# Attention's other TensorE work at fixed places, and each group's output projection in the group behind it

## The chip, the cores and the metric

The kernel runs on one NeuronCore of a Trainium2 chip. A core has five engines, each with its own queue of instructions in program order: PE (matrix multiply, with its weight loads shown apart as PEld), DVE (vector work), ACT (exp, gelu and copies), POOL (a second vector engine that cannot read PSUM), and SP, which here only issues DMA. Matmuls write PSUM, eight banks of 128 x 512 float32 numbers. The metric is the device time of one execution in microseconds; the time of a kernel is the median of its runs.

## The reference

One layer of 2048 tokens with 448 features. A gate per token mixes attention (16 heads of 28, one shared key and value head) with a shifted MLP block:

```python
def _A_ref(x, wq, wk, wv, wo):
    q = (x @ wq).reshape(B, S, H, Dh).transpose(0, 2, 1, 3)
    k = x @ wk
    v = x @ wv
    scores = jnp.einsum("bhqd,bkd->bhqk", q, k) * (Dh ** -0.5)
    p = _softmax(scores, axis=-1)
    o = jnp.einsum("bhqk,bkd->bhqd", p, v)
    return o.transpose(0, 2, 1, 3).reshape(B, S, H * Dh) @ wo

g = _sigmoid((x * gate_w).sum(-1, keepdims=True))
return g * _A_ref(x, wq, wk, wv, wo) + (1 - g) * _B_ref(x, w1, w2, w3, w4)
```

`_B_ref` is a layernorm, a product with w1, gelu, shifts of the tokens by one and two, a product with w2 and a sum with x, then a second layernorm and an MLP with w3 and w4.

## The kernel before, in words

The MLP block comes first and leaves its result in `x1`, already multiplied by 1 - g. The attention behind it is what the change touches.

Numbers that need full precision are split in a high and a low part of a rounded type (names ending in h and l); a product is then three matmuls. A **group** u is one of 16 pairs of a query block b (512 tokens) and a set g of four heads, u = 4b + g. For each group there are:

- **q**: `q_job` makes the queries of a group with 11 matmuls of 512 columns into one PSUM tile. `q_evac` then splits the tile (ACT copies `qh`, DVE subtracts to `ql`) and three DMAs on SP write them to `q_of[u]`.
- **m**: `max_part` makes scores of 128 keys only, four matmuls of 128 columns for one token tile t, and DVE takes their largest (L167). After four such sets `max_end` makes `mc` on DVE, and `max_rows` turns it with one matmul (`mt`), ACT copies it to `mrow`, and two small DMAs write it as further rows of `q_of[u]`, so that the score matmul subtracts it.
- **s and p**: for each of the 16 key tiles kt and each of the four heads j one matmul gives scores `s` (128 keys x 512 queries), and ACT takes exp of them to `p`.
- **pv**: `pv_group` adds the product of p with the values (and a column of ones) to one PSUM tile for the whole group. It is written for two key tiles at a time, behind the second of a pair, and with the p of the pair before (`LAG`, `PVB`). A float32 matmul shows as two records, so a pair has 16 of them.
- **norm**: when a group's pv is complete, `recip_begin` copies the tile to `o` (ACT), moves the row sums by DMA (`rt`), takes reciprocals on DVE and moves them back by two DMAs (`rb`). `norm_job` spreads them over the rows with one matmul (`rbc`), DVE multiplies, and POOL splits the product in `onh` and `onl`.
- **wo**: the output projection of a query block takes, for each token tile t and each of four groups g, three matmuls of 448 columns.

PE's order in attention is the order in which the program is written (the schedule of PE is manual); the other engines keep each its own queue, ordered by the framework. The loop over k runs through all key tiles of all groups, k = 16u + kt. Work that is not s, p or pv is a generator in the list `jobs`, and each call of `pump` writes one of its matmuls:

```python
if j % 2 == 1 or u == NU - 1:
    pump()
```

So `pump` (L600) is called twice in each key tile, in the last group four times. A q job is put ahead of the list at kt = 2 of each group (7 in the first); a norm job joins it six key tiles after its pv, and a block's four wo jobs (`wo_job`, L566) eight after the pv of its fourth group. A job's end takes a call of `pump` of its own. The m sets stand behind key tiles 6 to 9, `max_rows` behind 11 (L668 to L674).

`wo_job` adds all four groups of a block in one PSUM tile, 12 matmuls, and `gate_out` (L561) multiplies by the gate, adds `x1` and issues the output's DMA. For the last block this is done otherwise: `wo_last_job` (L638) keeps four PSUM tiles for its four token tiles over the whole last group, taken from the banks of `m_tile` and `s_more`, and adds groups 0 to 2 of the block into them during that group; the tail behind the loop adds the fourth.

PSUM in attention: two banks each for `mm_tile` and `s_more` and one for `s_spare` hold s in turn (in the last group only the first and the last of these, three banks: `s_tile`, L477), one bank holds pv, and two banks of `m_tile` serve q, m, mt, rbc and wo.

Of the kernel before, what the change touches and what calls it, by code (L numbers as in the profile page):

```python
# [8 lines left out]
F32 = mybir.dt.float32  # L9
F32R = mybir.dt.float32r  # L10
AF = mybir.ActivationFunctionType
ALU = mybir.AluOpType
# [3 lines left out]
P = 128  # L16
S = 2048
D = 448
# [4 lines left out]
NB = S // 512  # L23
NT = S // P
NF = F // P
NG = H // 4
# [14 lines left out]
def gated_mix_kernel(  # L41
# [13 lines left out]
    nc = tc.nc  # L55
# [11 lines left out]
    x1 = keep.tile([P, NT, D], F32, name="x1")  # L67
# [3 lines left out]
    gg = keep.tile([P, NT], F32, name="gg")  # L71
# [20 lines left out]
    def misc_tile(name):  # L92
        return psA.tile([P, 512], F32, tag="misc", bufs=1, name=name)
# [59 lines left out]
    NU = NB * NG  # L153
# [299 lines left out]
    with tc.tile_pool(name="s3", bufs=1, reuse_waits="tile") as s3, \  # L453
# [8 lines left out]
        woh = s3.tile([P, 4, D], F32R, name="woh")  # L462
# [11 lines left out]
        def s_spare(name):  # L474
            return psA.tile([P, 512], F32, tag="misc", bufs=1, name=name)

        def s_tile(n, last=False):  # L477
            return (mm_tile, mm_tile, s_spare, s_more, s_more)[n % (3 if last else 5)](f"s_{n}")

        xact = {}  # L480

# [10 lines left out]
        def q_job(u):  # L492
            b, g = divmod(u, NG)
            ah, al = xact[b]
            cols = slice(g * P, (g + 1) * P)
            ps = misc_tile(f"q_{u}")
            ops = []
            for c in range(3):
                ops += [(wqh[:, c, cols], ah[:, c, :]), (wqh[:, c, cols], al[:, c, :]), (wql[:, c, cols], ah[:, c, :])]
            ops += [(wqh[:, 3, cols], ah[:, 3, :]), (wql[:, 3, cols], ah[:, 3, :])]  # L500
            for n, (w, a) in enumerate(ops):
                nc.tensor.matmul(ps, w, a, start=(n == 0), stop=(n == 10))  # L502
# [10 lines left out]
        on_of = {}  # L513
# [23 lines left out]
            nc.sync.dma_start(f32(rb)[4:8, :].rearrange("j (a b) -> j a b", b=16), f32(rl))  # L537
            return o, rb

        def norm_job(u, o, rb):  # L540
            ps = (mm_tile if u == NU - 2 else misc_tile)(f"rbc_{u}")
            nc.tensor.matmul(ps, sel8, rb, start=True, stop=True)
            on = s3.tile([P, 512], F32, tag="onf", bufs=2, name=f"on_{u}")
            nc.vector.tensor_mul(on, o, ps)  # L544
            onh = s3.tile([P, 512], F32R, tag="onh", bufs=5, name=f"onh_{u}")
            onl = s3.tile([P, 512], F32R, tag="onl", bufs=5, name=f"onl_{u}")
# [5 lines left out]
        def wo_group(ps, b, t, g, first, last):  # L552
            tok = slice(t * P, (t + 1) * P)
            onh, onl = on_of[b * NG + g]
            nc.tensor.matmul(ps, onh[:, tok], woh[:, g, :], start=first, stop=False)  # L555
# [3 lines left out]
            nc.tensor.matmul(ps, onl[:, tok], woh[:, g, :], start=False, stop=last)  # L559

        def gate_out(n, ps):  # L561
            ot = s3.tile([P, D], F32, tag="ot", bufs=3, name=f"ot_{n}")
            nc.vector.scalar_tensor_tensor(ot, ps, gg[:, n:n + 1], x1[:, n, :], op0=ALU.mult, op1=ALU.add)  # L563
            nc.sync.dma_start(out[0, n * P:(n + 1) * P, :], ot)

        def wo_job(b, t):  # L566
            ps = misc_tile(f"wo_{b}_{t}")[:, 0:D]
            for g in range(NG):
                yield from wo_group(ps, b, t, g, g == 0, g == NG - 1)
                if g < NG - 1:  # L570
                    yield
            gate_out(4 * b + t, ps)
            yield

        wqraw = s3.tile([P, 4, 512], F32, tag="raw", bufs=2, name="wqraw")
        nc.sync.dma_start(wqraw, wq)
# [20 lines left out]
        jobs = []  # L597
        current = [None]

        def pump():  # L600
            if current[0] is None:
                if jobs:
                    current[0] = jobs.pop(0)()
                    next(current[0])
            else:
                try:
                    next(current[0])
                except StopIteration:
                    current[0] = None

        def drain():
            while current[0] is not None or jobs:
                pump()

        p_of, pv_of = {}, {}

        def pv_group(k):
            u, kt = divmod(k, NT)
            if kt == 0:
                pv_of[u] = max_tile(f"pv_{u}")  # L620
            pv = pv_of[u]
            ps = p_of.pop(k)
            for j in range(4):
                nc.tensor.matmul(pv[32 * j:32 * j + 32, :], vext[:, kt, :], ps[j],  # L624
                                 start=(kt == 0), stop=(kt == NT - 1), tile_position=(0, 32 * j))
            if kt == NT - 1 and u < NU - 1:
                o, rb = recip_begin(u, pv_of.pop(u))
                delayed.append((k + 6, lambda: norm_job(u, o, rb)))
                if u == NU - 2:
                    for t in range(4):  # L630
                        delayed.append((k + 10, lambda t=t: wo_last_job(t, NG - 2)))
                elif u % NG == NG - 1:
                    for t in range(4):
                        delayed.append((k + 8, lambda t=t: wo_job(u // NG, t)))

        wo_last = []

        def wo_last_job(t, g):  # L638
            if g == 0:
                wo_last.append((m_tile if t < 2 else s_more)(f"wo_{NB - 1}_{t}")[:, 0:D])  # L640
            yield from wo_group(wo_last[t], NB - 1, t, g, g == 0, False)
            yield

        delayed = []
        for k in range(NU * NT + LAG):
            u, kt = divmod(k, NT)
            while delayed and delayed[0][0] <= k:
                jobs.append(delayed.pop(0)[1])
            if k == (NU - 1) * NT:
                for g in range(NG - 2):  # L650
                    for t in range(4):
                        jobs.append(lambda t=t, g=g: wo_last_job(t, g))
            if k < NU * NT:
                if kt == (7 if u == 0 else 2) and u + 2 < NU:
                    jobs.insert(0, lambda u=u: q_job(u + 2))
                if kt == 8 and (u + 3) % NG == 0 and u + 3 < NU:
                    load_x((u + 3) // NG)
                p_of[k] = []
                for j in range(4):
                    n = 4 * k + j  # L660
                    ps = s_tile(n, u == NU - 1)
                    nc.tensor.matmul(ps, kS[0:98, kt * P:(kt + 1) * P], q_of[u][0:98, j, :], start=True, stop=True)  # L662
                    p = s3.tile([P, 512], F32, tag="p", bufs=4 * (LAG + PVB) + 2, name=f"p_{n}")
                    nc.scalar.activation(p, ps, AF.Exp, scale=SCALE)  # L664
                    p_of[k].append(p)
                    if j % 2 == 1 or u == NU - 1:
                        pump()
                if u + 1 < NU:  # L668
                    if 6 <= kt < 10:
                        max_part(u + 1, kt - 6, m_tile)  # L670
                    elif kt == 10:
                        max_end(u + 1)
                    elif kt == 11:
                        max_rows(u + 1, m_tile)  # L674
            if k >= LAG and k % PVB == PVB - 1:
                for kk in range(k - LAG - PVB + 1, k - LAG + 1):
                    if kk >= 0:
                        pv_group(kk)
        assert not delayed
        drain()  # L680

        u = NU - 1
        pv = pv_of.pop(u)
        o = s3.tile([P, 512], F32, tag="o", bufs=2, name=f"o_{u}")
        onh = s3.tile([P, 512], F32R, tag="onh", bufs=5, name=f"onh_{u}")
        onl = s3.tile([P, 512], F32R, tag="onl", bufs=5, name=f"onl_{u}")
        on_of[u] = (onh, onl)
        toks = [slice(t * P, (t + 1) * P) for t in range(4)]
        on4 = {}
# [15 lines left out]
            nc.vector.tensor_sub(onl[:, toks[t]], tq, f32(onh)[:, toks[t]])  # L705

        def tail_c(t):
            for _ in wo_group(wo_last[t], NB - 1, t, NG - 1, False, True):
                pass
            gate_out(4 * (NB - 1) + t, wo_last[t])  # L710

        for t in range(4):
            nc.scalar.copy(o[:, toks[t]], pv[:, toks[t]])
# [19 lines left out]
        with tc.If(again > 0):  # L733
            for b in range(NB):
                load_x(b)
                for g in range(NG):
# [7 lines left out]
                    for kt in range(NT):  # L744
                        for j in range(4):
# [7 lines left out]
                    for _ in norm_job(u, *recip_begin(u, pv, False)):  # L753
                        pass
                for t in range(4):
                    for _ in wo_job(b, t):
                        pass


_OUTS = [((1, S, D), "float32")]  # L760
# [48 lines left out]
```

## Time and profile before

| what | us |
|---|---|
| median of three runs | 1069.96 (1068.99 to 1070.19) |
| the profiled execution, its own time | 1067.96 |
| its span, first to last instruction | 1066.2 |
| PE busy in the span | 1040.3 |
| ACT busy in the span | 673.5 |
| attention, from the first s matmul to the end of the last pv | 420.57 to 1051.67 |

A line of a timeline has the start from the span's begin, the duration, engine, source line, operation, the tiles written and read, shapes, and the number of instructions that were merged; in brackets stands how long the engine was idle before it and what released it. A row of stretches has its limits and length, then for each of PE, PEld, DVE, ACT and POOL the busy time and (x) the number of instructions, then the clock that PE was granted, and the share and rate of DMA. A row of groups has busy time, mean duration in ns of one instruction, and the idle time before them with what ended it. Durations of matmuls overlap, so the time that a matmul takes of PE is read from start to start.

### The profile page before, as it was taken

The page shows a single profiled execution, that of the slowest core. Times are in us where ns is not written, and L with a number is a line of the kernel's source. Part 1 is how long each engine was busy: PE and PEld are TensorE (multiplying, and loading weights), DVE is VectorE, ACT ScalarE, POOL GpSimd, SP SyncE. Part 2 cuts the span into 40 slices and gives each one's busy share as a digit, 9 for nine tenths or more (in the row PEclk, how much of TensorE's full clock was granted, in tenths as well). Part 3 has the DMA queues.
Part 4 walks back from the last instruction along what each step waited for, and adds up shares of the span by engine and source line. Part 5 has one row for each costly group of instructions (what it writes and reads, how often), then busy time and mean ns, then how long its engine had stood idle before and what let it go on. Part 6 is the DMA issues. An engine that isn't in the chain of part 4 may idle for free.

```text
span 1066.2 us, 13945 instructions
## 1 busy us (share of the span) xinstructions
PE 1040.3 (98%) x5610; PEld 679.5 (64%) x5610; DVE 258.6 (24%) x528; ACT 673.5 (63%) x1318; POOL 146.1 (14%) x175
## 2 busy tenths in 40 slices
PE   7999989999999999999999999999999999999996
PEld 4787878888888887454554555554655555555442
DVE  6734862411412212301110110120110210111102
ACT  5444462222222223798888888889888888888873
POOL 5622200200200202602000002020002010000100
PEclk8899999999999999999999999999999999999998
DMA  9501330000000001323211202220202220202001
GB/s 312 133 1 37 112 111 1 1 1 1 1 1 1 1 1 61 132 32 70 32 18 15 31 19 41 39 31 3 39 10 41 39 31 2 40 21 30 10 2 38
DMA packets 30541, 41.15 MB, mean 39 GB/s; under 512 B 8004, under 2 KB 20100, under 8 KB 30340
## 3 DMA queue, kind: packets, MB, share of 16 engines
q1 hardware_dynamic: 30324, 40.04, 16.2%
q8 instruction: 46, 0.75, 0.3%
q14 instruction: 27, 0.22, 0.1%
q10 hardware_dynamic: 144, 0.13, 0.0%
HBM read 23.28 MB, written 3.67 MB: 25 GB/s over the span
## 4 chain that ended last, share of the span: by engine, by line
PE 92%; DVE 2%; DMA 2%; ACT 1%; POOL 1%; issue 1%; SPq 0%; POOLq 0%; DVEq 0%; ACTq 0%
PE s L662 27%; PE pv L624 22%; PE acc L418 4%; PE acc L419 4%; PE acc L420 4%; PE g L115 4%; PE g L116 4%; PE g L117 4%; PE q L502 3%; PE m L166 2%; PE wo L559 1%; PE wo L557 1%; PE g L119 1%; PE wo L555 1%; PE g L118 1%; PE h L116 1%
## 5 line engine op out<-in xcount | busy, mean ns | idle before, releaser
L664 ACT ACTIVATE p<-s 128x512 f32<-128x512 f32 x1024 | 517.6, 630 | 99.7 <-PE s L662 99.4
L662 PE MATMUL s<-qs,kS 98*128 98x512 f32 x1024 | 343.5, 420 | 1.4 <-ACT p L664 0.7
L662 PEld LDWEIGHTS s<-qs,kS 98*128 98x128 f32 x1024 | 181.7, 189 | 168.3 <-ACT p L664 126.2
L624 PE MATMUL pv<-p,vext 128*32 128x512 f32 x2048 | 247.5, 601 | 0.0
L408 ACT ACTIVATE gh<-g 128x512 fp32r<-128x512 f32 x56 | 33.6, 599 | 175.0 <-PE g L119 174.9
L624 PEld LDWEIGHTS pv<-p,vext 128*32 128x32 f32 x2048 | 53.7, 109 | 107.5 <-issue 100.1
L410 DVE TENSOR_TENSOR gl<-gf,gh 128x512 fp32r<-128x512 f32 x56 | 38.7, 692 | 183.8 <-ACT gf L409 183.8
L418 PE MATMUL acc<-w4h,gh 128*128 128x448 f32 x224 | 82.8, 370 | 0.0
L419 PE MATMUL acc<-w4l,gh 128*128 128x448 f32 x224 | 82.0, 366 | 0.0
L420 PE MATMUL acc<-w4h,gl 128*128 128x448 f32 x224 | 81.7, 365 | 0.0
L167 DVE TENSOR_REDUCE mr<-m 128x4 f32<-128x512 f32 x64 | 44.2, 691 | 146.8 <-PE m L166 146.1
L115 PE MATMUL g<-ah,w3h 128*128 128x512 f32 x168 | 66.6, 396 | 3.7 <-ACT gf L409 3.7
L116 PE MATMUL g<-al,w3h 128*128 128x512 f32 x168 | 66.3, 395 | 0.0
L117 PE MATMUL g<-ah,w3l 128*128 128x512 f32 x168 | 66.3, 394 | 0.0
L547 POOL CAST onh<-on 128x512 fp32r<-128x512 f32 x15 | 9.2, 614 | 415.0 <-DVE on L544 228.9
L520 DVE SCALAR_TENSOR_TENSOR good<-rt,good 128x16 f32<-128x16 f32 x15 | 2.6, 175 | 190.9 <-DMA rt<-o 190.9
L418 PEld LDWEIGHTS acc<-w4h,gh 128*128 128x128 f32 x224 | 42.2, 188 | 4.9
L419 PEld LDWEIGHTS acc<-w4l,gh 128*128 128x128 f32 x224 | 42.2, 188 | 4.9
L420 PEld LDWEIGHTS acc<-w4h,gl 128*128 128x128 f32 x224 | 42.0, 188 | 3.6
L166 PEld LDWEIGHTS m<-kS,qs 96*128 96x128 f32 x256 | 38.4, 191 | 6.3 <-DVE mr L167 1.2
L115 PEld LDWEIGHTS g<-ah,w3h 128*128 128x128 f32 x168 | 31.7, 188 | 9.9 <-ACT gf L409 4.1
L563 DVE SCALAR_TENSOR_TENSOR ot<-wo,gg,x 128x448 f32<-128x448 f32 x16 | 10.9, 681 | 108.0 <-PE wo L559 107.9
(204 smaller groups left out, 1134.9 us busy)
## 6 DMA issues: line engine op xcount, KB each, us to landing
qs<-qh SPq DMA_DIRECT2D x32, 256.0 KB
qs<-ql SPq DMA_DIRECT2D x16, 256.0 KB
xq<-in_xT_dram SPq DMA_DIRECT2D x4, 1024.0 KB
x<-in_x_dram SPq DMA_DIRECT2D x4, 896.0 KB
w3raw<-in_w_dram SPq DMA_DIRECT2D x7, 512.0 KB
out_dram<-ot SPq DMA_DIRECT2D x16, 224.0 KB
w4raw<-in_w_dram SPq DMA_DIRECT2D x7, 448.0 KB
xkv<-in_xT_dram SPq DMA_DIRECT2D x3, 1024.0 KB
```

Of the source, the lines that this page charges most:

```text
L115: nc.tensor.matmul(ps, wh[:, c, :], ah[:, c, :], start=(c == 0), stop=False)
L116: nc.tensor.matmul(ps, wh[:, c, :], al[:, c, :], start=False, stop=False)
L117: nc.tensor.matmul(ps, wl[:, c, :], ah[:, c, :], start=False, stop=False)
L166: nc.tensor.matmul(ps[:, j, :], q_of[u][0:96, j, t * P:(t + 1) * P], kS[0:96, 0:MK], start=True, stop=True)
L167: nc.vector.reduce_max(mx_of[u][:, :, t], ps, axis=AX.X)
L410: nc.vector.tensor_sub(gl, gf, f32(gh))
L418: nc.tensor.matmul(ps, gh[:, tok], w4h[i][:, k, :], start=(f == 0), stop=False)
L419: nc.tensor.matmul(ps, gh[:, tok], w4l[i][:, k, :], start=False, stop=False)
L420: nc.tensor.matmul(ps, gl[:, tok], w4h[i][:, k, :], start=False, stop=(f == NF - 1))
L624: nc.tensor.matmul(pv[32 * j:32 * j + 32, :], vext[:, kt, :], ps[j], start=(kt == 0), stop=(kt == NT - 1), tile_position=(0, 32 * j))
L662: nc.tensor.matmul(ps, kS[0:98, kt * P:(kt + 1) * P], q_of[u][0:98, j, :], start=True, stop=True)
L664: nc.scalar.activation(p, ps, AF.Exp, scale=SCALE)
```

## The change

`wo_job` now makes the projection of one group and one token tile, three matmuls in a PSUM tile of its own, and DVE adds the gated result to `ot` (the first group of a block adds to `x1`); the DMA of the output follows the fourth group. `wo_group`, `gate_out`, `wo_last_job` and the special case of the last block are gone, and s keeps its five banks to the end. Norm is no job any more but stands at key tile 6 of the next group, behind the second s. A job's last matmul no longer takes a further call of `pump`. `pump` is called at the places that `slots` names: behind the fourth s of every key tile and behind the second s of seven of them, 23 calls in a group, the number of 11 q and 12 wo matmuls. A group's q job starts at its key tile 0 (9 in the first group) and the wo jobs of the group before it at key tile 8. The m sets stand behind key tiles 3, 5, 7 and 9 and `max_rows` behind 11; in the first group behind 0, 1, 2, 3 and 6. PE's number of instructions is the same, DVE has 48 more for the adds in the part that runs. `onh` and `onl` have two buffers instead of five, `ot` five instead of three.

```diff
-        def s_tile(n, last=False):
-            return (mm_tile, mm_tile, s_spare, s_more, s_more)[n % (3 if last else 5)](f"s_{n}")
+        def s_tile(n):
+            return (mm_tile, mm_tile, s_spare, s_more, s_more)[n % 5](f"s_{n}")
...
-        def norm_job(u, o, rb):
-            ps = (mm_tile if u == NU - 2 else misc_tile)(f"rbc_{u}")
+        def norm(u, o, rb):
+            ps = misc_tile(f"rbc_{u}")
             nc.tensor.matmul(ps, sel8, rb, start=True, stop=True)
...
-        def wo_job(b, t):
-            ps = misc_tile(f"wo_{b}_{t}")[:, 0:D]
-            for g in range(NG):
-                yield from wo_group(ps, b, t, g, g == 0, g == NG - 1)
-                if g < NG - 1:
-                    yield
-            gate_out(4 * b + t, ps)
-            yield
+        def wo_job(u, t, tile_of=misc_tile):
+            b, g = divmod(u, NG)
+            n = 4 * b + t
+            tok = slice(t * P, (t + 1) * P)
+            onh, onl = on_of[u]
+            ps = tile_of(f"wo_{u}_{t}")[:, 0:D]
+            nc.tensor.matmul(ps, onh[:, tok], woh[:, g, :], start=True, stop=False)
             yield
             nc.tensor.matmul(ps, onh[:, tok], wol[:, g, :], start=False, stop=False)
             yield
+            nc.tensor.matmul(ps, onl[:, tok], woh[:, g, :], start=False, stop=True)
+            before = x1[:, n, :] if g == 0 else ot_of[n]
+            if g == 0:
+                ot_of[n] = s3.tile([P, D], F32, tag="ot", bufs=5, name=f"ot_{n}")
+            nc.vector.scalar_tensor_tensor(ot_of[n], ps, gg[:, n:n + 1], before, op0=ALU.mult, op1=ALU.add)
+            if g == NG - 1:
+                nc.sync.dma_start(out[0, n * P:(n + 1) * P, :], ot_of[n])
...
         def pump():
-            if current[0] is None:
-                if jobs:
-                    current[0] = jobs.pop(0)()
-                    next(current[0])
-            else:
-                try:
-                    next(current[0])
-                except StopIteration:
+            if jobs or current[0]:
+                current[0] = current[0] or jobs.pop(0)
+                if next(current[0], "done") == "done":
                     current[0] = None
...
+        def slots(u, kt):
+            if u == 0:
+                two = kt in (9, 11, 13, 15)
+                return () if kt < 9 else ((1, 3) if two else (3,))
+            return (1, 3) if kt in (0, 3, 7, 9, 11, 13, 15) else (3,)
+
+        def m_places(u):
+            return (0, 1, 2, 3, 6) if u == 0 else (3, 5, 7, 9, 11)
+
         for k in range(NU * NT + LAG):
             u, kt = divmod(k, NT)
...
+            if k < NU * NT:
+                if kt == (9 if u == 0 else 0) and u + 2 < NU:
+                    jobs.append(q_job(u + 2))
+                if kt == 8 and u > 0:
+                    for t in range(4):
+                        jobs.append(wo_job(u - 1, t))
...
-                    if j % 2 == 1 or u == NU - 1:
+                    if j in slots(u, kt):
                         pump()
-                if u + 1 < NU:
-                    if 6 <= kt < 10:
-                        max_part(u + 1, kt - 6, m_tile)
-                    elif kt == 10:
+                    if kt == 6 and j == 1 and norms:
+                        norm(*norms.pop())
+                if u + 1 < NU and kt in m_places(u):
+                    t = m_places(u).index(kt)
+                    if t < 4:
+                        max_part(u + 1, t, m_tile)
+                    else:
+                        max_rows(u + 1, m_tile)
+                    if t == 3:
                         max_end(u + 1)
-                    elif kt == 11:
-                        max_rows(u + 1, m_tile)
```

More of the change, by code (lines that the diff above doesn't have):

```diff
@@ L544, in norm_job @@
             nc.vector.tensor_mul(on, o, ps)
-            onh = s3.tile([P, 512], F32R, tag="onh", bufs=5, name=f"onh_{u}")
-            onl = s3.tile([P, 512], F32R, tag="onl", bufs=5, name=f"onl_{u}")
+            onh = s3.tile([P, 512], F32R, tag="onh", bufs=2, name=f"onh_{u}")
+            onl = s3.tile([P, 512], F32R, tag="onl", bufs=2, name=f"onl_{u}")
             nc.gpsimd.tensor_copy(onh, on)
@@ L549, in norm_job @@
             on_of[u] = (onh, onl)
-            yield
-        def wo_group(ps, b, t, g, first, last):
+        ot_of = {}
+        def wo_job(u, t, tile_of=misc_tile):
+            b, g = divmod(u, NG)
+            n = 4 * b + t
             tok = slice(t * P, (t + 1) * P)
-            onh, onl = on_of[b * NG + g]
-            nc.tensor.matmul(ps, onh[:, tok], woh[:, g, :], start=first, stop=False)
+            onh, onl = on_of[u]
+            ps = tile_of(f"wo_{u}_{t}")[:, 0:D]
+            nc.tensor.matmul(ps, onh[:, tok], woh[:, g, :], start=True, stop=False)
             yield
@@ L600, in pump @@
         def pump():
-            if current[0] is None:
-                if jobs:
-                    current[0] = jobs.pop(0)()
-                    next(current[0])
-            else:
-                try:
-                    next(current[0])
-                except StopIteration:
+            if jobs or current[0]:
+                current[0] = current[0] or jobs.pop(0)
+                if next(current[0], "done") == "done":
                     current[0] = None
[L611 to L615, printed above, removed]
+        p_of, pv_of, norms = {}, {}, []
         def pv_group(k):
@@ L626, in pv_group @@
             if kt == NT - 1 and u < NU - 1:
[L627 to L644, printed above, removed]
+                norms.append((u, *recip_begin(u, pv_of.pop(u))))
+        def slots(u, kt):
[5 more added lines that the diff above has]
+            return (0, 1, 2, 3, 6) if u == 0 else (3, 5, 7, 9, 11)
         for k in range(NU * NT + LAG):
             u, kt = divmod(k, NT)
[L647 to L650, printed above, removed]
+            if k < NU * NT:
+                if kt == (9 if u == 0 else 0) and u + 2 < NU:
+                    jobs.append(q_job(u + 2))
+                if kt == 8 and u > 0:
                     for t in range(4):
[L652 to L655, printed above, removed]
+                        jobs.append(wo_job(u - 1, t))
                 if kt == 8 and (u + 3) % NG == 0 and u + 3 < NU:
@@ L660, in gated_mix_kernel @@
                     n = 4 * k + j
-                    ps = s_tile(n, u == NU - 1)
+                    ps = s_tile(n)
                     nc.tensor.matmul(ps, kS[0:98, kt * P:(kt + 1) * P], q_of[u][0:98, j, :], start=True, stop=True)
@@ L678, in gated_mix_kernel @@
                         pv_group(kk)
-        assert not delayed
-        drain()
+        while current[0] or jobs:
+            pump()
+        assert not norms
         u = NU - 1
@@ L684, in gated_mix_kernel @@
         o = s3.tile([P, 512], F32, tag="o", bufs=2, name=f"o_{u}")
-        onh = s3.tile([P, 512], F32R, tag="onh", bufs=5, name=f"onh_{u}")
-        onl = s3.tile([P, 512], F32R, tag="onl", bufs=5, name=f"onl_{u}")
+        onh = s3.tile([P, 512], F32R, tag="onh", bufs=2, name=f"onh_{u}")
+        onl = s3.tile([P, 512], F32R, tag="onl", bufs=2, name=f"onl_{u}")
         on_of[u] = (onh, onl)
@@ L707, in tail_c @@
         def tail_c(t):
-            for _ in wo_group(wo_last[t], NB - 1, t, NG - 1, False, True):
+            for _ in wo_job(u, t, m_tile if t < 2 else s_more):
                 pass
-            gate_out(4 * (NB - 1) + t, wo_last[t])
         for t in range(4):
@@ L752, in gated_mix_kernel @@
                                              start=(kt == 0), stop=(kt == NT - 1), tile_position=(0, 32 * j))
[L753 to L757, printed above, removed]
+                    norm(u, *recip_begin(u, pv, False))
+                    for t in range(4):
+                        for _ in wo_job(u, t):
+                            pass
 _OUTS = [((1, S, D), "float32")]
```

7 lines of the change are left out of this document (removed).

## The prediction

> **What bounds the kernel now.** I read the page first, then busy time by stretch, then PE's timeline pair by pair.
>
> ```profile
> span 1066.2 us, 13945 instructions
> PE 1040.3 (98%) x5610; PEld 679.5 (64%) x5610; DVE 258.6 (24%) x528; ACT 673.5 (63%) x1318; POOL 146.1 (14%) x175
> ```
>
> PE looks full. The stretches below are group 0, groups 1 to 13 together, group 14 and group 15 up to its last pv matmul (a group is one u: 512 queries of four heads).
>
> ```profile
> 420.57:461.81 41.24, 39.36 (x206) 18.90 (x204) 12.59 (x16) 32.54 (x66) 21.76 (x16) 0.96 0.50 144
> 461.81:967.29 505.48, 505.48 (x3004) 274.19 (x3000) 72.89 (x165) 432.31 (x872) 42.75 (x33) 1.00 0.18 29
> 967.29:1005.69 38.40, 38.40 (x231) 20.30 (x227) 7.61 (x14) 32.64 (x66) 3.78 (x4) 1.00 0.04 14
> 1005.69:1051.67 45.98, 45.06 (x249) 20.96 (x245) 1.38 (x5) 32.92 (x66) 1.89 (x2) 1.00 0.01 1
> ```
>
> Attention is 631 of the 1066 us. Its columns are length, then busy time of PE, weight load, DVE, ACT, POOL. A middle group takes 505.48 / 13 = 38.88 us, group 15 takes 7 us more, and PE is "busy" without a gap from group 1 to group 14. That busy time hides waiting, as a pair of key tiles with no other work shows (eight s, then pv, then the next pair's s; below it the s weight loads of this pair alone, from the groups by line):
>
> ```profile
> 490.90 2.66 PE L662 MATMUL s<-qs,kS 98*128 98x512 f32 x8
> 493.49 1.92 PE L624 MATMUL pv<-p,vext 128*32 128x512 f32 x16
> 495.35 0.50 PE L662 MATMUL s<-qs,kS 98*128 98x512 f32 x1
> L662 PEld LDWEIGHTS s<-qs,kS 98*128 98x128 f32 x8 | 1.4, 187 | 1.8 <-ACT p L664 1.6
> ```
>
> It takes 4.45 us, and its s weight loads stood 1.6 us behind exp: five PSUM banks hold s, so the seventh and eighth s wait until the second and third exp have let their bank go. **So 4.45 us is the floor of a pair**, set by exp and pv together, and work put ahead of the eighth s fills that wait; work behind it comes on top. Rows of fuller pairs (start, duration, count; "..." leaves out the rest of a pair):
>
> ```profile
> 610.47 0.72 PE L662 MATMUL s<-qs,kS 98*128 98x512 f32 x2
> ...
> 612.97 0.36 PE L555 MATMUL wo<-woh,onh 128*128 128x448 f32 x1
> 613.27 1.92 PE L624 MATMUL pv<-p,vext 128*32 128x512 f32 x16
> 615.12 0.50 PE L662 MATMUL s<-qs,kS 98*128 98x512 f32 x1
> ```
>
> Two wo matmuls ahead of the eighth s and one behind: 4.65 us, the behind one starting at 2.50. Two cost nothing, the third 0.20.
>
> ```profile
> 466.26 0.73 PE L662 MATMUL s<-qs,kS 98*128 98x512 f32 x2
> ...
> 471.10 0.50 PE L662 MATMUL s<-qs,kS 98*128 98x512 f32 x1
> ```
>
> Three q matmuls ahead, one behind: 4.84.
>
> ```profile
> 659.46 1.20 PE L662 MATMUL s<-qs,kS 98*128 98x512 f32 x4
> ...
> 662.06 0.39 PE L502 MATMUL q<-ahq,wql 128*128 128x512 f32 x1
> 664.23 0.50 PE L662 MATMUL s<-qs,kS 98*128 98x512 f32 x1
> ```
>
> Two q ahead, one behind, in the second pair of a group, where ACT also copies o: 4.77. From the last q to the next pair are 2.17 us.
>
> ```profile
> 632.26 0.40 PE L502 MATMUL q<-ahq,wqh 128*128 128x512 f32 x1
> 632.50 0.56 PE L166 MATMUL m<-kS,qs 96*128 96x128 f32 x4
> 634.84 0.50 PE L662 MATMUL s<-qs,kS 98*128 98x512 f32 x1
> ```
>
> With a set of four m behind the q they are 2.58: a set behind the eighth s costs 0.41, and a q step is 632.50 - 632.26 = 0.24.
>
> **Groups 1 to 13.** PE's instructions keep their number and size; their places change. In a group's pairs P0 to P7 the new order has: P0 two q ahead, one behind: 4.84 - 0.24 = 4.60. P1 two q ahead, one and an m set behind, o copied: 4.77 + 0.41 = 5.18. P2 one q ahead, one and a set behind: the eighth s is held to the same point as in the wo pair, so the q starts at about 2.50, 2.50 + 2.58 = 5.08. P3 rbc and two q ahead, one and a set behind (rbc taken as a q, both are 128x512): 4.84 + 0.41 = 5.25. P4 two wo ahead, one and a set behind: 4.65 + 0.41 = 5.06. P5 the same with mt instead of the set, a quarter of its matmuls: 4.65 + 0.10 = 4.75. P6 and P7: 4.65 each. The sum is 39.22, against 38.88 now: 13 x 0.34 = **4.4 us more**. They hold 13 groups' projections instead of 12, and the last piece of every pair stands behind the eighth s, where the floor does not hide it, while now two to four pairs in many groups carry nothing.
>
> **Group 14** has no q now or then: P0 4.45, P1 4.45 + 0.41 + 0.08 for the o copy (4.77 - 4.65, less 0.04 that a q is longer than a wo), P2 and P3 4.86 each (rbc is hidden), then P4 to P7 as above: 38.2 against 38.40, **0.2 less**.
>
> **Group 15** loses 24 of its 36 wo matmuls to groups 13 and 14, and s gets five banks back instead of three:
>
> ```profile
> 1005.69 0.50 PE L662 MATMUL s<-qs,kS 98*128 98x512 f32 x1
> ...
> 1011.12 0.50 PE L662 MATMUL s<-qs,kS 98*128 98x512 f32 x1
> 1048.04 3.64 PE L624 MATMUL pv<-p,vext 128*32 128x512 f32 x32
> ```
>
> A pair with six wo and three banks takes 5.43. New: P0 to P3 at the floor and 0.08 for o, 17.88; P4 to P6 at 4.65, 13.95; P7 613.27 - 610.47 = 2.80 up to pv and 3.64 of pv, 6.44. The sum is 38.3 against 45.98: **7.7 less**, the largest term.
>
> **Group 0.** It starts with pairs held back by exp alone; later PE waits for q's operand, and then runs at half clock:
>
> ```profile
> 420.57 6.49 PE L662 MATMUL s<-qs,kS 98*128 98x512 f32 x16
> 428.85 2.66 PE L662 MATMUL s<-qs,kS 98*128 98x512 f32 x8
> 432.11 1.64 DVE L487 CAST ahq<-xq 128x2048 fp32r<-128x2048 f32 x1
> 437.50 0.50 PE L502 MATMUL q<-alq,wqh 128*128 128x512 f32 x1 [1.40 <-POOL alq L488]
> 445.77 0.69 DVE L167 TENSOR_REDUCE mr<-m 128x4 f32<-128x512 f32 x1 [1.15 <-PE m L166]
> 446.70 0.18 DVE L186 SCALAR_TENSOR_TENSOR mc<-mr,mc 128x16 fp32r<-128x16 f32 x1
> 435.19:438.59 3.40, 2.00 (x13) 1.26 (x16) 0.58 (x2) 2.67 (x6) 3.32 (x2) 1.00 0.50 193
> 438.60:442.00 3.40, 3.40 (x17) 0.75 (x10) 0.53 (x1) 0.00 (x0) 3.25 (x3) 0.50 0.47 151
> ```
>
> New: the first two pairs last 8.28 as now, three m sets lie in their waits, the fourth behind the last s: 8.69. P2 is empty, 4.45. In P3 mt stands in the middle, and waits for mc. On DVE m's third reduction now stands behind the wq casts, where the ahq cast began at 432.11, and its fourth behind that cast: 432.11 + 0.69 + 1.64 + 0.69 + the 0.42 from the end of a reduction to the end of L186 = 435.5. PE arrives at 420.57 + 8.69 + 4.45 + about 1.0 for four s (1.20 in the q pair above, less what the last overlaps) = 434.7. The wait of 0.8, and a weight load of 0.19 after it, takes the place of the old 1.40; behind mt stand four s, then pv, and exp waits for those s. About 0.4 is what the s waits would have taken anyway: P3 4.45 + 0.65 = 5.1. Q is now wanted at 440, when POOL's alq (it ended at 437.50) is done. P4 to P7 carry at most two q ahead and one behind, without o: 4.69 each. The sum is 8.69 + 4.45 + 5.1 + 18.8 = 37.0 against 41.24: **4.2 less**.
>
> **What else moves, and who covers it.**
>
> ```profile
> L563 DVE SCALAR_TENSOR_TENSOR ot<-wo,gg,x 128x448 f32<-128x448 f32 x16 | 10.9, 681 | 108.0 <-PE wo L559 107.9
> 454.50:461.50 7.00, 6.52 (x42) 2.44 (x41) 0.69 (x1) 6.58 (x15) 0.00 (x0) 1.00 0.81 112
> 461.50:463.90 2.40, 2.40 (x11) 1.23 (x7) 0.00 (x0) 1.98 (x5) 0.00 (x0) 1.00 0.00 0
> ```
>
> Each projection is now its own PSUM sum, added on DVE: 48 more adds of 0.68, 33 us, on an engine busy 72.89 of 505 us; one per pair from P4 on, some 3 us before the next tile starts. Without that cover each costs up to 0.68. POOL's onh and onl move to P3 with rbc, a pair ahead of wo. Rbc at P3 needs rb, whose transfers are issued in P1, two pairs ahead. On DVE the check of rt waits for a DMA in P1 with m's first reduction queued behind it; the next m wants a bank a pair later. Out keeps its 16 transfers on SP, between mrow's, after waits that P6 and P7 cover. The tightest is group 0's last q: its copies kept DMA busy until about 461.5, 7 us after the ACT copy; in the new order that lands some 2.6 us into P1 of group 1, about when m first reads it: 0 to 2 us, once; I take 0.
>
> **Sum:** -4.2 + 4.4 - 0.2 - 7.7 = -7.7. The profiled execution took 1067.96 (span 1066.2) and would take 1060.3; the median of the runs is 1069.96, 2.0 above it, so **1062.3 us**. The tail behind the last pv keeps its work.
>
> **Rivals.** *Half clock again* (0.20). In the stretch above PE was granted 0.50 for 3.4 us, right behind the wait of 1.40: 1.7 us lost. The new wait for mt is shorter, but if the clock falls, 1064.0. The Trainium skill (TensorE: Matmul & The Clock Gate, Part 1) says that the half rate comes after at least one idle window of about 3.4 us; by that, a wait of this size never costs clock and the sum stays 1062.3. This trace disagrees: PE was busy for 2.00 of the 3.40 us before.
>
> *PE bound throughout* (0.07): busy 505.48 of 505.48 and equal matmuls would leave 1070. The 1.6 us of weight loads waiting in an empty pair, and three wo for 0.20, speak against it.
>
> *A slower kernel* (0.06): the two m banks serve q, m, mt, rbc and wo, and now each wo tile must leave through DVE before the bank is used again. Were the adds of 60 tiles on PE's path, less the 0.44 that a pair hides (two wo steps), 60 x 0.24 = 14 us on 1062.3: 1077. It decides from (1069.96 - 1062.3) / 60 = 0.13 us a tile. Against it: a tile's third matmul stands 2.50 into a pair and the next tile's first behind the fourth s of the next, some 3 us later.
>
> *The middle groups stay at 38.88* (0.07), since P1 to P5 hide more than the rows of single pairs let me think: 1058.
>
> **How the numbers follow.** The forecast has 0.60. Unknown costs: the m sets and pieces behind an already held s, 0.15 a group either way, 2 us; the mt wait, from none (-0.65) to the old one (+0.6); group 1's DMA, up to 2; the clock, 1.7. The range is 1059.5 to 1066.0; it leaves out the slower kernel, no change and most of 1058. Within 0.2% (2.1 us, about what a measurement of this kernel can tell from no change) is 1067.8 to 1072.1. Faster 0.60 + 0.20 + 0.07 = 0.87, same 0.07, slower 0.06.
>
> **What would show it.** In the new profile: pairs of group 15 at 4.45 and 4.65 instead of 5.43; a middle group at 39.2; PE's wait before mt in group 0 near 0.8 us, and the clock there; no wait of wo on DVE. Wrong it would be if middle groups ran over 39.8 us, or if m of group 1 or rbc waited for DMA in every group.

## The result and the profile after

The changed kernel takes 1067.01 us (median of 20 runs, 1065.87 to 1069.64); the kernel before, run beside it, 1068.59 (20 runs, 1066.86 to 1070.79). The ratio is 0.9986, with a 95% interval of 0.9979 to 0.9992: faster by 0.14%, less than the 0.2% named as the bound of no change, and above the range of the forecast. The forecast stood on 1069.96, the median of three runs, which lies 1.4 above that of the 20; by the difference, 1.6 us were won and not 7.7. The profiled execution took 1067.31, its span is the first line here. PE and DVE stand in the second line, the new adds of wo in the third (lines of the page of the kernel after).

```profile
span 1065.5 us, 14021 instructions
PE 1035.8 (97%) x5610; PEld 677.6 (64%) x5610; DVE 294.7 (28%) x576; ACT 673.5 (63%) x1318; POOL 145.9 (14%) x175
L566 DVE SCALAR_TENSOR_TENSOR ot<-wo,gg,ot 128x448 f32<-128x448 f32 x48 | 32.8, 684 | 156.4 <-PE wo L562 156.4
```

Next the busy time by stretch of the same execution: group 0, group 1, groups 2 to 13 together, group 14, group 15.

```profile
421.36:462.27 40.91, 37.68 (x205) 18.22 (x203) 14.27 (x15) 32.56 (x66) 21.76 (x16) 0.96 0.37 126
462.27:502.59 40.32, 39.47 (x237) 21.28 (x233) 9.40 (x17) 33.61 (x68) 8.51 (x5) 1.00 0.37 67
502.59:973.61 471.02, 471.02 (x2801) 256.23 (x2797) 95.67 (x192) 398.86 (x804) 35.95 (x30) 1.00 0.18 28
973.61:1011.74 38.13, 38.13 (x227) 19.29 (x223) 7.00 (x15) 32.76 (x66) 1.89 (x2) 1.00 0.01 2
1011.74:1050.01 38.27, 38.27 (x225) 17.39 (x221) 4.11 (x9) 32.69 (x65) 1.90 (x2) 1.00 0.01 2
```

| group | before | forecast | after |
|---|---|---|---|
| 0 | 41.24 | 37.0 | 40.91 |
| 1 to 13 | 505.48 | 509.9 | 511.34 |
| 14 | 38.40 | 38.2 | 38.13 |
| 15 | 45.98 | 38.3 | 38.27 |
| attention | 631.10 | 623.4 | 628.65 |

Three of the five stretches came out as forecast: groups 2 to 13, with 471.02 / 12 = 39.25 us each, group 14 and group 15. Group 0 nearly kept its time, and group 1 has 1.1 too much. So attention became 2.45 us shorter, not 7.7. In the two profiled spans 0.79 us of that is lost ahead of attention (it starts at 421.36 instead of 420.57), and about 1.0 behind it. The program ahead of attention is the same in all eleven profiles of this case, and attention starts at 420.0 to 422.4 us in them, so the 0.79 lies within what differs from run to run. From the end of the last pv to the end of the span are 14.5 us in the kernel before and 14.7 to 15.6 in the ten profiles with the new tail; how much of the 1.0 is the change's is not shown.

PE's waits in attention, added up by what ended them (total, times, longest), are only two, and they lie in groups 0 and 1; no add of wo is among them, nor among the waits of the weight loads, where those of s for exp stand (120.2 us in all):

```profile
PE mt L193 <- DVE mc L186: 3.2, 1, 3.2
PE m L166 <- DMA qs<-qh: 0.8, 1, 0.8
```

**Group 0.** The timeline of PE, of DVE and of POOL in the fourth pair (P3) of the kernel after:

```profile
434.47 1.20 PE L638 MATMUL s<-qs,kS 98*128 98x512 f32 x4
438.90 0.30 PE L193 MATMUL mt<-identR,mc 128*128 128x128 f32 x1 [3.23 <-DVE mc L186]
439.03 1.63 PE L638 MATMUL s<-qs,kS 98*128 98x512 f32 x4
440.59 3.04 PE L610 MATMUL pv<-p,vext 128*32 128x512 f32 x16
443.56 1.70 PE L638 MATMUL s<-qs,kS 98*128 98x512 f32 x6
```

```profile
434.76 0.68 DVE L167 TENSOR_REDUCE mr<-m 128x4 f32<-128x512 f32 x1
435.48 3.06 DVE L185 TENSOR_SCALAR mc<-mr 128x16 fp32r<-128x16 f32 x1
438.58 0.18 DVE L186 SCALAR_TENSOR_TENSOR mc<-mr,mc 128x16 fp32r<-128x16 f32 x1
```

```profile
435.08 3.43 POOL L488 TENSOR_TENSOR alq<-xq,ahq 128x1536 fp32r<-128x1536 f32 x1 [1.62 <-PE s L638]
```

PE waited for mt 3.23 us, and the wait is DVE's: L185, which reads 16 numbers a partition, took 3.06 us, and ended at 438.54, 0.03 after POOL's `alq` (435.08 + 3.43 = 438.51). The profile shows this as the instruction's duration, not as a wait. Over all groups its shortest, median and longest time are 174, 175 and 3058 ns:

```profile
L185 DVE TENSOR_SCALAR mc<-mr x16: 174/175/3058, 172.5 to 996.9; 128x16 fp32r<-128x16 f32 x16
```

In groups 1, 5 and 9 it took 1.11 to 1.16 us beside POOL's L489 (1.27 us), each time to 0.03 us behind that instruction's end; PE did not wait for it there. Behind the wait PE ran at half clock, and pv took 3.04 instead of 1.92 (clock is the third number from the right in the stretches):

```profile
436.07:439.47 3.40, 0.57 (x3) 0.56 (x4) 2.65 (x2) 1.24 (x4) 3.32 (x2) 1.00 0.47 179
439.47:442.88 3.41, 3.41 (x16) 0.98 (x18) 0.00 (x0) 2.08 (x5) 3.26 (x3) 0.50 0.41 126
```

P3 so runs from 434.47 to 443.56, 9.09 us: the floor of 4.45, 3.23 of waiting, 1.7 of clock, less a remainder of 0.3, put down to s waits that would have been there anyway.

**Group 1.** In P1 the first m waits for the copies of group 0's last q (PE's timeline; PE stood idle for 0.85, and the pair took 6.25 instead of the 5.17 of the same pair in group 3):

```profile
470.79 0.63 PE L166 MATMUL m<-kS,qs 96*128 96x128 f32 x4 [0.85 <-DMA qs<-qh]
471.36 1.92 PE L610 MATMUL pv<-p,vext 128*32 128x512 f32 x16
```

### The profile page after: what moved, and what is told of

Same layout as the page of the kernel before. It is cut to its first block, busy times and chain, and to the rows that moved or that the text cites. A ratio compares the mean times of both kernels' runs of the same rounds, so it can differ in the third digit from the quotient of the medians.

```text
span 1065.5 us, 14021 instructions
## 1 busy us (share of the span) xinstructions
PE 1035.8 (97%) x5610; PEld 677.6 (64%) x5610; DVE 294.7 (28%) x576; ACT 673.5 (63%) x1318; POOL 145.9 (14%) x175
## 4 chain that ended last, share of the span: by engine, by line
PE 90%; DVE 3%; DMA 3%; ACT 2%; issue 0%; POOL 0%; SPq 0%; DVEq 0%; POOLq 0%
PE s L638 25%; PE pv L610 22%; PE acc L418 4%; PE acc L419 4%; PE acc L420 4%; PE g L115 4%; PE g L116 4%; PE g L117 4%; PE q L502 3%; PE m L166 2%; PE wo L558 1%; PE g L119 1%; PE wo L560 1%; PE g L118 1%; PE wo L562 1%; PE h L116 1%
## 5 line engine op out<-in xcount | busy, mean ns | idle before, releaser
L638 PE MATMUL s<-qs,kS 98*128 98x512 f32 x1024 | 331.4, 421 | 0.0
L638 PEld LDWEIGHTS s<-qs,kS 98*128 98x128 f32 x1024 | 183.0, 188 | 171.4 <-ACT p L640 120.2
L566 DVE SCALAR_TENSOR_TENSOR ot<-wo,gg,ot 128x448 f32<-128x448 f32 x48 | 32.8, 684 | 156.4 <-PE wo L562 156.4
L167 DVE TENSOR_REDUCE mr<-m 128x4 f32<-128x512 f32 x64 | 44.2, 690 | 87.1 <-PE m L166 87.1
```

Source lines behind the costliest of these rows:

```text
L167: nc.vector.reduce_max(mx_of[u][:, :, t], ps, axis=AX.X)
```

## The experiments

Each is an edit of the kernel after. Pair and group lengths are read from PE's timeline, from the first s of one to the first s of the next.

**What holds L185: its form, or POOL?** The same result made with two SBUF operands in another instruction:

```diff
-        nc.vector.tensor_scalar(mc[:, 0:16], mr, -1.0, None, op0=ALU.mult)
+        nc.vector.scalar_tensor_tensor(mc[:, 0:16], mr, 0.0, mr, op0=ALU.mult, op1=ALU.subtract)
```

> The first instruction of max_end, which in the changed kernel takes 3.06 us in group 0 instead of 0.17 while POOL makes alq, becomes a scalar_tensor_tensor with two SBUF inputs, the form of the second one. Theory, port: any DVE instruction with two reads from SBUF stands back while POOL runs; then it still takes about 3 us in group 0, PE waits 3.2 us before mt and the pair stays near 9.1 us. Rival, mode: only the form of a tensor with constants is held up by POOL; then it takes 0.2 us, mc is ready at about 435.9, PE waits 0.5 to 0.9 us, the pair is near 5.1 and group 0 near 37.0 instead of 40.9. Rival, queue: DVE itself is late and the duration only shows a wait; then nothing changes either, and m's fourth reduction is late too.

One run took 1067.81. L185 again took 3.06 us and ended with `alq` (DVE's and POOL's timeline):

```profile
434.61 3.06 DVE L185 SCALAR_TENSOR_TENSOR mc<-mr 128x16 fp32r<-128x16 f32 x1
```

```profile
434.20 3.43 POOL L488 TENSOR_TENSOR alq<-xq,ahq 128x1536 fp32r<-128x1536 f32 x1 [1.63 <-PE s L638]
```

Between these two forms there is no difference, so the rival that only a fast mode of `tensor_scalar` is held falls. Group 0 took 42.31, since the half clock lasted twice as long:

```profile
437.68:441.09 3.41, 3.06 (x13) 1.59 (x16) 0.18 (x1) 2.30 (x5) 3.22 (x3) 0.50 0.17 56
441.10:444.51 3.41, 3.41 (x18) 1.00 (x11) 0.00 (x0) 0.01 (x1) 3.41 (x1) 0.50 0.77 256
```

**A POOL instruction in three pieces.** `alq` of block 0 is made 512 columns at a time:

```diff
-            nc.gpsimd.tensor_tensor(al, raw[:, 0:3, :], f32(ah)[:, 0:3, :], ALU.subtract)
+            for c in [slice(0, 3)] if b else [slice(i, i + 1) for i in range(3)]:
+                nc.gpsimd.tensor_tensor(al[:, c, :], raw[:, c, :], f32(ah)[:, c, :], ALU.subtract)
```

> POOL makes alq of the first query block in three pieces of 512 columns instead of one of 1536. Theory, port: the DVE instruction gets through at the end of a piece, so it takes at most 1.2 us, mc is ready near 436.6, PE waits about 1.2 us, and the pair takes 5.4 to 6; if a wait of that size is enough for the clock to fall, 1.7 us more. Rival, mode or queue: it has nothing to do with the length of POOL's instruction, and takes 3 us as before.

One run took 1067.4, and group 0 39.87. The timelines of DVE and of POOL (whose line numbers are one higher here):

```profile
436.53 0.90 DVE L185 TENSOR_SCALAR mc<-mr 128x16 fp32r<-128x16 f32 x1
437.47 1.19 DVE L186 SCALAR_TENSOR_TENSOR mc<-mr,mc 128x16 fp32r<-128x16 f32 x1
```

```profile
436.12 3.74 POOL L489 TENSOR_TENSOR alq<-xq,ahq 128x512 fp32r<-128x512 f32 x3 [1.63 <-PE s L639]
```

A piece is 3.74 / 3 = 1.25 us. L185, begun 0.41 into the first, ended at 437.43, near that piece's end; L186, begun then, stood behind the second. So the hold lasts as long as the POOL instruction that runs, which shows POOL as the cause. The pair took 8.03 us, not the 5.4 to 6 expected, because I had not seen that L186 would be held as well: the wait for mt was 2.11 us, and the clock still fell for 3.4 us.

**The wait taken away.** `max_rows` of group 0 two key tiles later, so that PE asks for mc after `alq` is done:

```diff
-            return (0, 1, 2, 3, 6) if u == 0 else (3, 5, 7, 9, 11)
+            return (0, 1, 2, 3, 8) if u == 0 else (3, 5, 7, 9, 11)
```

> Only in group 0, mt stands behind key tile 8 instead of 6, 2.5 us behind the point at which mc was ready; nothing else is changed. Theory: the long DVE instruction stays (3 us), but PE does not wait for it, so P3 is an empty pair of 4.45, mt lies in P4 (4.7), the clock is granted in full throughout, and group 0 takes 36.4 us instead of 40.9; the kernel gains 4.5 us, 1062.5. Rival, clock by another cause (DMA, POOL, the cast of wq): PE keeps the 3.4 us at half clock near 440 us, 1.7 us of loss remain, group 0 takes about 38.1.

The time is 1061.86 (4 runs, 1061.12 to 1064.07), 0.9934 of before (0.9911 to 0.9957). L185 is still held, for 3.12 us, but nothing waits for it, and the clock stays whole over group 0:

```profile
420.56:456.83 36.27, 36.27 (x205) 18.06 (x203) 14.30 (x15) 32.29 (x66) 21.84 (x16) 1.00 0.42 142
```

Group 0 is 40.91 - 36.27 = 4.64 us shorter: that was the price of one hold, wait and clock together.

**Group 1's wait for the copies.** First, m later in group 1 (key tiles 5, 6, 7, 9 instead of 3, 5, 7, 9):

```diff
-            return (0, 1, 2, 3, 6) if u == 0 else (3, 5, 7, 9, 11)
+            return (0, 1, 2, 3, 6) if u == 0 else (5, 6, 7, 9, 11) if u == 1 else (3, 5, 7, 9, 11)
```

> Only in group 1, the m sets stand behind key tiles 5, 6, 7 and 9 instead of 3, 5, 7 and 9. Theory, DMA: in P1 of group 1 PE waited 1.1 us for the three transfers of group 2's q; with a pair more the wait is gone, P1 takes 4.77 instead of 6.25, P2 5.08, P3 5.65 with a second set, and the group 39.25 instead of 40.32. Rival, bank: PE waited for DVE to free a bank of m; then the wait moves with the first set and P2 takes over 6 us.

One run took 1066.78. The wait in P1 is gone, with 4.77, but P3 grew to 6.73, and group 1 took 40.32 as in the kernel after. The first reduction of m now stands ahead of `rl` on DVE, and waits for PE; `rl` comes 4.5 us after `rh`, its transfer too, and `rbc` waits; the m set behind it waits 0.15 more, for the DVE instruction that reads `rbc` (timelines of DVE and of PE):

```profile
471.23 0.17 DVE L532 CAST rh<-rr 128x16 fp32r<-128x16 f32 x1
475.17 0.69 DVE L167 TENSOR_REDUCE mr<-m 128x4 f32<-128x512 f32 x1 [3.77 <-PE m L166]
475.77 0.17 DVE L533 TENSOR_TENSOR rl<-rr,rh 128x16 fp32r<-128x16 f32 x1
```

```profile
478.04 0.47 PE L541 MATMUL rbc<-rb,sel 128*128 128x512 f32 x1 [0.39 <-DMA rb<-rl]
```

The other way, group 0's q earlier, in P4 to P6, with mt moved as above:

```diff
-                two = kt in (9, 11, 13, 15)
-                return () if kt < 9 else ((1, 3) if two else (3,))
+                return () if kt < 8 or kt > 13 else ((1, 3) if kt > 8 else (3,))
...
-                if kt == (9 if u == 0 else 0) and u + 2 < NU:
+                if kt == (8 if u == 0 else 0) and u + 2 < NU:
```

> The changed kernel with mt of group 0 behind key tile 8 and group 0's q done in P4 to P6 (three, four and four steps), a pair earlier; the other groups are left as they are. Theory, DMA: the transfers of group 2's q end a pair earlier, PE does not wait in P1 of group 1, which takes 5.17 instead of 6.25 to 6.31, and group 0 takes 36.4 to 36.6: 1060.9. Rival, queue: the wait in P1 is for DVE, whose queue holds the check of rt ahead of m's reduction; then it stays.

The time is 1060.62 (4 runs, 1059.87 to 1061.04), 0.9931 of before (0.9913 to 0.9948). P1 of group 1 takes 5.17 and the group 39.23, 1.09 less than after. Group 0 took 36.44.

**Where group 15's 7.7 us came from.** The new order, but s in three banks during group 15, as before:

```diff
-            return (mm_tile, mm_tile, s_spare, s_more, s_more)[n % 5](f"s_{n}")
+            return (mm_tile, mm_tile, s_spare, s_more, s_more)[n % (5 if n < 64 * (NU - 1) else 3)](f"s_{n}")
```

> The changed kernel with s in three PSUM banks instead of five in group 15, as in the kernel before; the 12 wo matmuls of that group stay. Theory, banks: a pair of group 15 takes 5.4 us with or without wo, as the kernel before has it, so group 15 takes 7.2 us more, 45.5 instead of 38.27. Rival, wo: the 24 wo matmuls that the change took out of group 15 were the 7.7 us; then it stays near 38.3 to 39.

One run took 1076.8. Group 15 and a stretch in its third pair:

```profile
1012.54:1060.35 47.81, 46.16 (x225) 16.89 (x221) 4.11 (x9) 32.69 (x65) 1.88 (x2) 0.96 0.01 1
1023.90:1027.20 3.30, 3.08 (x12) 1.18 (x14) 0.00 (x0) 3.18 (x7) 0.00 (x0) 0.99 0.00 0
1027.20:1030.60 3.40, 3.40 (x16) 0.46 (x11) 0.00 (x0) 0.85 (x2) 0.00 (x0) 0.51 0.00 0
```

Pairs with no wo at all take 5.43, the same as pairs with six took before; those with three, one of them behind the eighth s, take 5.62 or 5.63. Without the 1.7 us of half clock group 15 is 46.1, before 45.98. So the gain there is that of the two banks; with three banks the 24 wo matmuls that left lay in waits. What all 36 would cost beside five banks, no run shows.

**All steps ahead of the eighth s.** In the order of the kernel after, the third piece of a pair stands behind the eighth s. With the slots of groups 1 to 15 moved forward:

```diff
-            return (1, 3) if kt in (0, 3, 7, 9, 11, 13, 15) else (3,)
+            return (3,) if kt == 4 else (1,) if kt % 2 else (1, 3)
```

> The changed kernel with one edit: in groups 1 to 15 the three steps of a pair stand behind the second, fourth and sixth s instead of two ahead and one behind the eighth. Theory, floor: work ahead of the eighth s fills the wait for exp, work behind it comes on top: P6 and P7 take 4.53 instead of 4.65, P2 4.78 instead of 5.08, P3 stays at 5.25, a middle group takes 38.3 instead of 39.25; the kernel gains 13 to 14 us, 1053.5, with the 9.1 us pair of group 0 and the wait of group 1 still there. Rival, PE bound: the same matmuls in other places, a group stays at 39.25.

The time is 1053.24 (4 runs, 1053.13 to 1055.96), 0.986 of before (0.9843 to 0.9877). A middle group takes 38.26 to 38.39, some 0.9 less in each of 12, and group 1 is 0.8 shorter. The profiled execution was the slowest of the four, 1055.96, the others 1053.1 to 1053.3. Group 0 took 42.35 in it, with PE again 3.25 us behind mc, and then half clock for 6.8 us.

**All three moves:** mt of group 0 behind its key tile 8, its q from there on and ahead of the eighth s (`m_places` and the start of q as shown above), and the slots of the last run.

```diff
-                two = kt in (9, 11, 13, 15)
-                return () if kt < 9 else ((1, 3) if two else (3,))
-            return (1, 3) if kt in (0, 3, 7, 9, 11, 13, 15) else (3,)
+                return {8: (1, 3), 9: (1, 2), 10: (1, 3), 11: (1, 2), 12: (1, 3), 13: (1,)}.get(kt, ())
+            return (3,) if kt == 4 else (1,) if kt % 2 else (1, 3)
```

> The version that the runs point to: mt of group 0 behind key tile 8, group 0's q in its pairs P4 to P6 (four, four and three steps) instead of P4 to P7, and in all other groups the three steps of a pair behind the second, fourth and sixth s, none behind the eighth. Theory: group 0 about 36.4 us at full clock, no wait of PE for DMA in P1 of group 1, a middle group 38.3 us instead of 39.25, group 14 37.6, group 15 37.8: 12 x 1.0 + 2.0 + 0.5 + 0.5 + 4.5 = 19.5 less than the changed kernel, 1047.5. Rival, PE bound: only the 4.5 us of group 0 and the 1.1 of group 1 are won, 1061.5. Rival, new wait: a step that now comes earlier finds its operand late (mc held by POOL in groups 1, 5 and 9, or the wait of wo for onl), which shows as idle PE in P4 or P5 of those groups, 1 to 3 us each.

The time is 1047.92 (5 runs, 1047.2 to 1049.02), 0.981 of before (0.9794 to 0.9826); no other version here is as fast. Groups 0, 1 and 2 to 13 (460.08 / 12 = 38.34):

```profile
420.54:456.95 36.41, 36.41 (x205) 18.35 (x203) 15.05 (x16) 32.54 (x66) 21.89 (x16) 1.00 0.53 158
456.95:495.26 38.31, 38.31 (x237) 21.84 (x233) 7.85 (x16) 33.35 (x68) 8.53 (x5) 1.00 0.29 55
495.26:955.34 460.08, 460.08 (x2801) 262.17 (x2797) 93.21 (x192) 399.00 (x805) 35.98 (x30) 1.00 0.18 29
```

**How much a pair can hide.** The kernel of the run above, with the m sets and mt of groups 1 to 14 behind the seventh s instead of the eighth:

```diff
-                if u + 1 < NU and kt in m_places(u):
+                    if j == (2 if u else 3) and u + 1 < NU and kt in m_places(u):
```

> The kernel of the run with all three moves, with the m sets and mt of groups 1 to 14 put behind the seventh s of a pair instead of the eighth. How much can a pair hide? If it is the 1.6 us that its s weight loads stand behind exp, three pieces of 0.24 and a set of 0.45 all fit, pairs P1 to P4 fall from 5.0, 4.84, 5.25 and 4.94 to some 4.6, a middle group from 38.3 to 36.8 and the time from 1047.9 to about 1027. If it is PE's own steps (eight s of 0.24 are 1.92 of the 2.59 us up to pv, so 0.67 is free, and three pieces have filled it), the sets cost the same ahead as behind: pairs within 0.1 but for P2, which has only two pieces and gains 0.1 to 0.2, a middle group 38.0 to 38.3, the time 1044 to 1048. A new wait, of m for a bank of m_tile or for DVE, would show as pairs over 5.3 and a time over 1050.

The time is 1051.33 (4 runs, 1050.0 to 1052.48), 0.9834 of before (0.9812 to 0.9855): none of the large gain. A pair with q and m, in full:

```profile
501.89 0.74 PE L637 MATMUL s<-qs,kS 98*128 98x512 f32 x2
502.46 0.40 PE L502 MATMUL q<-ahq,wqh 128*128 128x512 f32 x1
502.70 0.63 PE L637 MATMUL s<-qs,kS 98*128 98x512 f32 x2
503.17 0.40 PE L502 MATMUL q<-alq,wqh 128*128 128x512 f32 x1
503.41 0.63 PE L637 MATMUL s<-qs,kS 98*128 98x512 f32 x2
503.88 0.40 PE L502 MATMUL q<-ahq,wql 128*128 128x512 f32 x1
504.12 0.39 PE L637 MATMUL s<-qs,kS 98*128 98x512 f32 x1
504.35 0.56 PE L166 MATMUL m<-kS,qs 96*128 96x128 f32 x4
504.74 0.44 PE L637 MATMUL s<-qs,kS 98*128 98x512 f32 x1
505.12 1.92 PE L610 MATMUL pv<-p,vext 128*32 128x512 f32 x16
506.97 1.20 PE L637 MATMUL s<-qs,kS 98*128 98x512 f32 x4
```

Ten steps, seven s and three q, take 504.35 - 501.89 = 2.46, or 0.246 each: no step waits here any more. Eight such s and 1.86 of pv are 3.83, so of the floor of 4.45 only 0.62 can be filled, two and a half pieces, and not the 1.6 us for which the weight loads wait. Three pieces fill it, and m comes on top wherever it stands: 5.08 in this pair, 5.04 with m behind. In group 14, whose P1 to P3 have no q, the move did gain, 0.21 or 0.22 a pair (4.94 to 4.72, 4.85 to 4.63, 4.84 to 4.63). P2 of a middle group, with two pieces, was to gain 0.1 to 0.2 and stayed at 4.84; P1, P3, P4 and P5 became 0.02 to 0.09 longer. Middle groups took 38.51 to 38.56, and this profile's attention starts 1.8 us later. A P3 of 5.27 to 5.31 and a time over 1050 are the numbers named for a new wait, but PE has no wait in attention here; why the groups lost 0.2 is not settled.

## Why the forecast was wrong

**The step that failed is mc's date in group 0.** The sum "432.11 + 0.69 + 1.64 + 0.69 + the 0.42 from the end of a reduction to the end of L186 = 435.5" gave L185 and L186 the time that they had taken with POOL idle, and did not ask what POOL would run beside them. Counted from the start of attention, PE came when I said (434.7, and 0.79 later 435.5; measured 438.90 - 3.23 = 435.67), but mc was ready at 438.76 instead of 436.3, since L185 took 3.06 and not 0.17: PE waited 3.23 us and not 0.8. I had worked out that q no longer waits for `alq`, and had not asked what else `alq` would now lie beside. A sign stood in the sum itself: its 1.64 for the ahq cast is from a row that began under POOL's L582. In the kernel after, with POOL idle, the cast took 1.23. So DVE reached L185 0.4 us sooner than forecast, at 435.48; with 0.38 for L185 and L186 PE would have waited about 0.2, by estimate. Rows of DVE, then of POOL, in the kernel before, and the cast after:

```profile
434.92 0.69 DVE L167 TENSOR_REDUCE mr<-m 128x4 f32<-128x512 f32 x1 [1.17 <-PE m L166]
...
991.26 1.23 DVE L185 TENSOR_SCALAR mc<-mr 128x16 fp32r<-128x16 f32 x1
```

```profile
431.87 0.79 POOL L582 TENSOR_TENSOR wql<-wqraw,wqh 64x256 fp32r<-64x256 f32 x1
433.98 3.46 POOL L488 TENSOR_TENSOR alq<-xq,ahq 128x1536 fp32r<-128x1536 f32 x1 [1.32 <-PE s L662]
...
991.19 1.28 POOL L548 TENSOR_TENSOR onl<-on,onh 128x512 fp32r<-128x512 f32 x1
```

```profile
433.62 1.23 DVE L487 CAST ahq<-xq 128x2048 fp32r<-128x2048 f32 x1
```

L185 took 1.23 at 991.26, under POOL's L548, and ended with it, seven times its median of 0.175; PE did not wait for it there. The reduction L167, which reads PSUM, began 0.94 us into `alq` and took its usual 0.69. The Trainium skill (SBUF — State Buffer, section SBUF: two separate sides) states a rule for such a hold: VectorE in a fast two-port mode, or with two SBUF inputs against a GpSimd instruction that reads SBUF, and GpSimd share one pair of ports, and whoever starts first has it for its whole instruction. The 3.06 us, and the 0.90 and 1.19 of the run with pieces, agree with it; which of its two cases L185 is in its own form, no run here shows.

**The half clock** was a rival (0.20) at 1.7 us, and came, at that price; but it came behind a wait of 3.23, not of 0.8. By the Trainium skill's rule, weighed in the forecast (TensorE: Matmul & The Clock Gate, Part 1), it takes an idle window of about 3.4 us; the stretch ahead of the fall had 0.57 of 3.40 busy, nearer to that than the 2.00 before, but the 3.08 of 3.30 in the run with three banks is not. Wait and clock together made group 0 3.9 longer than forecast, and the run with mt moved gives back 4.6.

**Group 1's copies** were "0 to 2 us, once; I take 0", and cost 1.07. The end of the range had it; the value did not.

**Right:** the middle groups (39.22 forecast, 39.25), group 14 (38.2, 38.13) and group 15 (38.3, 38.27, and by the banks, as the run with three shows). The pairs of groups 2 to 13 came within 0.1: P0 4.69 for 4.60, P1 5.17 for 5.18, P2 5.08 for 5.08, P3 5.25 for 5.25, P4 5.05 for 5.06, P5 4.71 for 4.75, P6 and P7 4.65. So the rival that they stay at 38.88 fell. The slower rival fell too: the row of L566 has 156.4 us in which DVE waited for PE, and PE's waits hold none for an add. The time came out near the 1070 of the rival "PE bound throughout", but not by its mechanism: it would have left every stretch as it was, while group 15 lost 7.7 and groups 1 to 13 gained 5.9, and moving the pieces forward saves 0.9 a group. Once three pieces of a pair are forward, PE's own steps are its bound, as the run with m ahead shows.

With the two misses added the sum would have been -7.7 + 3.9 + 1.1 = -2.7, against -2.45 measured for attention. "The tail behind the last pv keeps its work" held for the work; the 1.0 us more behind it is open.

## What to carry to other kernels

When work is moved, list not only what it waits for but also what will run at the same time, here on POOL beside a DVE instruction: a duration taken from a quiet place is the price without that neighbour, and a row whose longest time is many times its median says where to look. Put small pieces ahead of the wait that they are to fill, and work out the room from the steps' own spacing, not from the wait that the weight loads show. Taking slack out of one queue's order can make a later transfer late, so a move against one wait is read against the whole group.

## What the runs showed of the hardware

A 128x16 DVE instruction took 3.06 us beside a 3.43 us POOL instruction, in both forms tried, and 0.90 beside one of 1.25; a reduction out of PSUM was not slowed beside one of 3.46 (0.69). The clock fell to half behind PE waits of 1.40 (before), 2.11, and 3.22 to 3.25 us, not behind the 0.85 in group 1; it stayed there for 3.4 us, and in two runs, with waits of 3.22 and 3.25, for 6.8. In these two the clock fell while PE still waited (0.35 and 0.07 us ahead of mt), in the others after PE had gone on; that this decides between 3.4 and 6.8 is not shown. In the run with three banks it fell behind a stretch in which PE was busy for 3.08 of 3.30 us, without a wait over 0.3; why there, and why only in one pair of that group, is open.
